# The bias of a spectral mixing, put into the PSUM bank by ScalarE instead of by a matmul

## The chip, the cores and the metric

The kernel runs on one core of a Trainium2 chip. The metric is the device time of one execution in microseconds (us). The kernel before took 1985.57 us, the median of three runs (1985.16 to 1986.27).

## What is computed

Three layers follow one another on a tensor of 4 batches, 3072 positions and 256 channels. The first takes a Fourier transform along the positions, mixes the channels of every frequency with a complex matrix and a bias, shrinks the result softly, and transforms back. The change lies in this layer alone. The reference, cut to it and to the order of the three:

```python
X = np.fft.rfft(x, axis=1)
Xr, Xi = X.real, X.imag
Yr = Xr @ w_r - Xi @ w_i + b_r
Yi = Xr @ w_i + Xi @ w_r + b_i
Yr = np.sign(Yr) * np.maximum(np.abs(Yr) - 0.01, 0.0)
Yi = np.sign(Yi) * np.maximum(np.abs(Yi) - 0.01, 0.0)
y = np.fft.irfft(Yr + 1j * Yi, n=3072, axis=1)
# y goes through moe (w_in, mish, w_out), then moe2 (w_k, relu squared, w_v, gate w_g)
```

## The kernel before

The program has two parts. `part1` is the Fourier layer, `part2` the other two layers. In both, every matrix product is made of products of high and low halves of its operands (names ending in h and l).

`part1` works on 48 blocks, 12 for each batch; a block is 128 frequencies of one batch. For block u TensorE does three groups of matmuls. `emit_F(u)` (F below) is the forward transform of 8 matmuls into the bank `xps`. `emit_M(u)` (M) is the mixing into the bank `yps`: 12 products and, last, one matmul of the constants `pick` and `bias` that adds the bias (L650). In every twelfth block (u = 0, 12, 24, 36, where `t` is 0) the mixing is split in two halves of 256 columns with a bias matmul each. `emit_I(u)` (I) is the inverse transform of 8 matmuls into `bps`. The order on TensorE in step u of the main loop (L736 to L800) is F(u+1), M(u), I(u-1).

ScalarE evacuates the banks. In step u it does, in this order: `post_M(u-1)` (reads `yps`, writes `yb`), `post_F(u+1)` (reads `xps`, writes `xh`), its share of decoding a weight, `post_I(u-2)` (reads `bps`, writes `bs`, which a DMA takes to `b_dr`), and in the last batch the share of a second weight. VectorE writes `xl` in `post_F` (called X below) and finishes `yb` in `post_M2` (called Y).

The weights of the later layers arrive as 64-bit floats and are decoded (`decode`, L446) in steps over both engines: VectorE `v0` (integer parts into `q`), ScalarE `sg` twice and `q`, VectorE `v1` (`q` times sign), ScalarE the high half, VectorE the low half. One piece is worked on per step for u from 6 to 14 (parked to DRAM through `wp` and `w_dr`) and two per step in the last batch (u from 36 on). Steps of different pieces overlap, so each `v1` waits for the `q` that ScalarE made just before.

VectorE also has work in the background, in a queue with a planner (`Background`, L353 to L410). It holds the butterflies before the transform of the next batch (tile `a`, due before that batch) and the butterflies after the inverse transform, called F3 here (tile `g`, two jobs of 48 entries for batch 0 in `part1`, one for each half of the channels, added at u = 16 and u = 20). The planner keeps a clock of its own in nanoseconds: TensorE's time `pe`, and VectorE's `bg.clock`. Ahead of each Y and X it emits background operations as long as their costs fit by its clock (`until`). A step of `pe` is 1710 for F, 2770 for M and 1710 for I (L767, L792, L796). Operations for `a` always go before those of F3 (`one`, `until`: `self.q or self.f3`). A new F3 job is loaded only when the job before it is empty, and may begin three steps after that (`step`, L368 to L374). What is left in the last batch is emitted at u = 46 (`drain`, L799), and then `load_y(0)` reads what F3 stored, for `part2`; `split_y` on VectorE comes after it and ahead of the last Y.

The order of each engine's instructions is the order in which this Python code emits them. SP issues all DMAs in one queue.

Of the kernel before, what the change touches and what calls it, by code (L numbers as in the profile page):

```python
# [10 lines left out]
F32 = mybir.dt.float32  # L11
F32R = mybir.dt.float32r
I32 = mybir.dt.int32
ACTF = mybir.ActivationFunctionType
# [15 lines left out]
NT = 12  # L30
# [83 lines left out]
def tile_fft_mix_moe_channel_mix(  # L114
# [23 lines left out]
    def pool(stack, name, bufs, **kw):  # L138
        return stack.enter_context(tc.tile_pool(name=name, bufs=bufs, reuse_waits="tile", **kw))
# [5 lines left out]
    def tt(o, a, b, op):  # L145
        V.tensor_tensor(out=o, in0=a, in1=b, op=op)  # L146
# [4 lines left out]
    def act(o, i, f, **kw):  # L151
        S.activation(out=o, in_=i, func=f, **kw)  # L152

    def mm(o, l, r, start, stop, **kw):
        T.matmul(out=o, lhsT=l, rhs=r, start=start, stop=stop, **kw)  # L155
# [97 lines left out]
    def both(a, z):  # L253

        return [e for pair in zip(a, z) for e in pair]
# [315 lines left out]
    def part1():  # L571
        with ExitStack() as es:
            c1 = pool(es, "c1", 1)
# [7 lines left out]
            psy = pool(es, "psy", 3, space=PSUM)  # L581
            psb = pool(es, "psb", 3, space=PSUM)

            fm, im = {}, {}
            bias = c1.tile([128, 512], F32R, name="bias")
            pick = c1.tile([128, 2, 128], F32R, name="pick")
            zero = c1.tile([128, 64], F32, name="zero")
            As = {}

            def new_a(b):  # L590
                As[b] = big.tile([128, 2, 32, 128], F32, tag="big", name="a")
                for h in range(2):
                    load_x(As[b], b, h)

            xt, ybt, xps, yps, bps = {}, {}, {}, {}, {}

            def emit_F(u):
                b, t = u // NT, ORD[u % NT]
                A = As[b]
                ps = psx.tile([128, 2, 256], F32, tag="x", name="xps")  # L600
                lr, li = LINES_F[t]
                line = lambda h, l: A[:, h, l, :]
                if b == 0 and t < 4:
                    line = lambda h, l: G0[:, 16 * h + LINES_G[l - 16], :]
                half = lambda z, i: z.rearrange("p (r i f) -> p r i f", r=2, i=2)[:, :, i, :]
                for h in range(2):
                    if t:
                        mm(ps[:, h, :], line(h, lr), fm[t][:, 0, :], True, False)
                        mm(ps[:, h, :], line(h, li), fm[t][:, 1, :], False, True)
                    else:  # L610
                        for i, l in enumerate((lr, li)):
                            mm(half(ps[:, h, :], i), line(h, l), half(fm[0][:, i, :], i), True, True)
                xps[u] = ps

            def post_F(u):
                t = u % NT
                ps = xps.pop(u)
                xh = xs_p.tile([128, 2, 256], F32R, tag="xh", name="xh")
                xl = xs_p.tile([128, 2, 256], F32R, tag="xl", name="xl")
                act(xh, ps, ACTF.Copy)  # L620
                tt(xl, ps, xh.bitcast(F32), SUB)
                xt[u] = (xh, xl)
                if t == 0:
                    zh = z_p.tile([128, 2, 256], F32R, tag="zh", name="zh")
                    zl = z_p.tile([128, 2, 256], F32R, tag="zl", name="zl")
                    for zz, xx in ((zh, xh), (zl, xl)):
                        S.activation(out=zz, in_=xx.bitcast(F32), func=ACTF.Copy)
                        S.activation(out=zz.rearrange("p h (r f) -> p (h r) f", r=2)[:, :, 0:1],
                                     in_=zero[:, 0:4].rearrange("p (a o) -> p a o", o=1), func=ACTF.Copy)
                    xt[u] += (zh, zl)  # L630

            def emit_M(u):
                t = u % NT
                ps = psy.tile([128, 512], F32, tag="y", name="yps")
                xs = xt.pop(u)
                if t:
                    groups = [(slice(0, 512), ((0, 256, 0), (1, 0, 0)))]
                else:

                    groups = [(slice(0, 256), ((0, 256, 0), (1, 0, 2))),  # L640
                              (slice(256, 512), ((0, 512, 2), (1, 256, 0)))]
                for gs, parts in groups:
                    n = gs.stop - gs.start
                    todo = []
                    for zl, lo in ((0, 0), (0, 1), (1, 0)):
                        for h in range(2):
                            w = wt["mix", h][lo]
                            for r, c0, z in parts:
                                todo.append((xs[z + zl][:, h, 128 * r:128 * r + 128], w[:, c0:c0 + n]))
                    todo.append((pick[:, 0 if t else 1, :], bias[:, gs]))  # L650
                    for i, (l, r) in enumerate(todo):
                        mm(ps[:, gs], l, r, i == 0, i == len(todo) - 1)
                yps[u] = ps


            def post_M(u):
# [69 lines left out]
            bg.add(both(z[8:], m[:4]) + m[4:])  # L726
            bg.flush()
            emit_F(0)
            post_F(0)
            bg.add(both(t0[0][1], t0[1][1]) + both(t0[0][2][:10], t0[1][2][:10]), 4)  # L730
            bg.add(both(t0[0][2][10:], t0[1][2][10:]), 8)
            NU = NB * NT

            pe, bg.clock = START
            x_at, y_at = bg.clock, 0.0
            for u in range(NU):  # L736
                b, t = divmod(u, NT)
                if t == NT - 1 and b + 2 < NB:
                    new_a(b + 2)
                if t == F1_AT[b] and b + 1 < NB:  # L740
                    hs = [f1_ops(As[b + 1], h) for h in range(2)]
                    for i, due in ((slice(14), 0), (slice(14, 24), 4), (slice(24, None), 8)):
                        bg.add(both(*[(h[0] + h[1])[i] for h in hs]), NT * (b + 1) + due)
                bg.jobs += F3_PART1.get((b, t), [])
                bg.step()
                if u == NU - NT - 1:
                    wt["in"] = big.tile([128, 2, 2, 2048], F32R, tag="big", name="win")
                    todo = [lambda: win_piece(0)]
                    for i in range(8):
                        if i < 7:  # L750
                            todo.append(lambda i=i: win_piece(i + 1))
                        todo.append(lambda i=i: wout_piece(i))
                    late = [lambda i=i: park_piece(i) for i in range(NPARK, 9)]
                    wq = Weights(todo[:6] + late + todo[6:])
                    wq.load(3)
                dec = 0
                if b == NB - 1:
                    dec = 2
                elif PARK_AT[0] <= u < PARK_AT[1]:
                    dec = 1  # L760
                    if u == PARK_AT[0]:
                        wq = Weights([lambda i=i: park_piece(i) for i in range(NPARK)])
                        wq.load(2)
                bg.flush(u + 1)
                if u == 6:
                    S.activation(out=mu1, in_=mu, func=ACTF.Copy, scale=-1.0, bias=1.0)
                pe += 1710 * (u + 1 < NU)  # L767
                if u + 1 < NU:
                    emit_F(u + 1)
                if u:  # L770
                    post_M(u - 1)
                if dec:
                    emit(wq.vec())
                    bg.clock += 2100
                if u:
                    bg.until(y_at + SLACK[0])
                    post_M2(u - 1)
                    y_at = bg.spend(y_at, 602)
                if u + 1 < NU:
                    bg.until(pe + 700 + SLACK[1])  # L780
                    post_F(u + 1)
                    x_next = bg.spend(pe + 700, 602)
                if dec:
                    emit(wq.sca(2))
                if u > 1:
                    post_I(u - 2)
                if dec == 2:
                    emit(wq.vec())
                    emit(wq.sca(2))
                    bg.clock += 2100  # L790
                emit_M(u)
                pe = max(pe, x_at + 300) + 2770  # L792
                y_new = pe + 700
                if u:
                    emit_I(u - 1)
                    pe = max(pe, y_at + 300) + 1710  # L796
                x_at, y_at = x_next, y_new
                if b == NB - 1 and t == 10:
                    bg.drain()  # L799
                    load_y(0)  # L800
# [267 lines left out]
```

## Time and profile before

| | us |
|---|---|
| median of three runs | 1985.57 |
| lowest, highest | 1985.16, 1986.27 |
| the profiled execution, its own time | 1985.22 |
| its span, first to last instruction | 1983.2 |
| TensorE busy in it | 1960.9 |
| VectorE busy | 1143.1 |
| ScalarE busy | 925.1 |

`part1` fills the first 327 us of the span, `part2` the rest. A busy share is a mean over stages with different limits; the ends of matmuls are modelled, so it is the distance from start to start that gives a matmul's price.

### The profile page before, as it was taken

How to read it: one execution, taken by the hardware profiler on the slowest of the kernel's cores; microseconds unless marked ns; L12 is line 12 of the kernel's file. 1: busy time of each engine (PE TensorE's matmuls, PEld its weight loads, DVE VectorE, ACT ScalarE, POOL GpSimd, SP SyncE). 2: the span in 40 equal slices, each digit the busy share in tenths (PEclk: the TensorE clock that was granted, in tenths of full speed). 3: DMA queues.
4: the chain of work that ended last, by engine and by line, in shares of the span. 5: the costliest groups of instructions: out<-in, count | busy, mean ns of one | idle time of the engine just before them, and what ended most of it. 6: DMA issues, size and time to landing. Idle time of an engine off the chain costs nothing.

```text
span 1983.2 us, 25749 instructions
## 1 busy us (share of the span) xinstructions
PE 1960.9 (99%) x10084; PEld 1687.4 (85%) x10084; DVE 1143.1 (58%) x2183; ACT 925.1 (47%) x1525; POOL 13.5 (1%) x28
## 2 busy tenths in 40 slices
PE   6999999999999999999999999999999999999999
PEld 5888888888888888888888888888888888888888
DVE  8999986655654764465375445555444543444444
ACT  2423286344444544444444445444443544444455
POOL 0000000000000000000000000000000000000000
PEclk9999999999999999999999999999999999999999
DMA  9445276011011010101101001011000000000000
GB/s 278 151 136 170 71 246 202 34 33 64 22 33 54 22 46 9 54 22 33 54 22 54 1 22 54 8 31 38 22 1 22 22 11 11 22 22 1 22 11 22
DMA packets 104553, 106.66 MB, mean 54 GB/s; under 512 B 7016, under 2 KB 85488, under 8 KB 103408
## 3 DMA queue, kind: packets, MB, share of 16 engines
q1 hardware_dynamic: 104432, 105.02, 16.7%
q8 instruction: 79, 1.29, 0.3%
q14 instruction: 42, 0.34, 0.1%
HBM read 62.53 MB, written 42.47 MB: 53 GB/s over the span
## 4 chain that ended last, share of the span: by engine, by line
PE 97%; DMA 1%; DVE 1%; ACT 1%; issue 0%; SPq 0%; DVEq 0%; ACTq 0%
PE a L155 26%; PE hps L155 26%; PE v L155 14%; PE kps L155 13%; PE yps L155 7%; PE bps L155 4%; PE xps L155 4%; PE zps L155 3%; DMA a<-in_x_dram 0%; DMA w_dr<-wp 0%; DMA wraw<-in_w_r_dram 0%; DMA im<-in_inv_dram 0%; ACT sg L152 0%; SPq L266 0%; DVE q L149 0%
## 5 line engine op out<-in xcount | busy, mean ns | idle before, releaser
L864 DVE CAST gh<-u 128x512 fp32r<-128x512 f32 x384 | 163.4, 425 | 685.1 <-PE a L155 594.3
L155 PE MATMUL a<-gh,wo 128*128 128x512 f32 x1536 | 536.7, 390 | 0.0
L155 PE MATMUL hps<-yh,win 128*128 128x512 f32 x1536 | 534.7, 389 | 0.0
L152 ACT ACTIVATE u<-hps 128x512 f32<-128x512 f32 x384 | 229.7, 598 | 483.1 <-PE hps L155 428.5
L155 PEld LDWEIGHTS hps<-yh,win 128*128 128x128 f32 x1536 | 288.4, 188 | 60.4
L155 PEld LDWEIGHTS a<-gh,wo 128*128 128x128 f32 x1536 | 288.6, 188 | 57.8
L155 PE MATMUL a<-gl,wo 128*128 128x512 f32 x768 | 300.1, 391 | 0.0
L155 PE MATMUL hps<-yl,win 128*128 128x512 f32 x768 | 298.8, 389 | 0.0
L155 PE MATMUL v<-b,kh 128*128 128x256 f32 x1536 | 279.8, 281 | 0.0
L146 DVE TENSOR_TENSOR gl<-u,gh 128x512 fp32r<-128x512 f32 x384 | 263.9, 687 | 3.6
L155 PEld LDWEIGHTS v<-b,kh 128*128 128x128 f32 x1536 | 249.6, 189 | 14.3
L155 PE MATMUL v<-b,kl 128*128 128x256 f32 x768 | 215.8, 281 | 0.0
L152 ACT ACTIVATE ka<-kps 128x512 f32<-128x512 f32 x192 | 114.8, 598 | 211.0 <-PE kps L155 210.9
L155 PEld LDWEIGHTS hps<-yl,win 128*128 128x128 f32 x768 | 144.2, 188 | 29.8
L155 PEld LDWEIGHTS a<-gl,wo 128*128 128x128 f32 x768 | 144.7, 188 | 25.7
L146 DVE TENSOR_TENSOR kl<-ka,kh 128x512 fp32r<-128x512 f32 x192 | 132.9, 692 | 44.0 <-ACT ka L152 29.4
L155 PE MATMUL kps<-xkl,wkt 128*128 128x512 f32 x384 | 150.7, 392 | 0.0
L155 PEld LDWEIGHTS v<-b,kl 128*128 128x128 f32 x768 | 144.2, 188 | 0.0
L155 PE MATMUL kps<-b,wkt 128*128 128x512 f32 x384 | 134.5, 391 | 0.0
L155 PE MATMUL kps<-xkh,wkt 128*128 128x512 f32 x384 | 134.0, 391 | 0.0
L152 ACT ACTIVATE ka<-ka 128x512 f32<-128x512 f32 x192 | 121.8, 634 | 6.1
L152 ACT ACTIVATE kh<-ka 128x512 fp32r<-128x512 f32 x192 | 121.6, 633 | 6.1
(80 smaller groups left out, 2069.8 us busy)
## 6 DMA issues: line engine op xcount, KB each, us to landing
b_dr<-bs SPq DMA_DIRECT2D x48, 256.0 KB, 2.2
g<-b_dr SPq DMA_DIRECT2D x8, 1536.0 KB, 6.7
y<-y_dr SPq DMA_DIRECT2D x48, 256.0 KB, 3.1
out_dram<-r SPq DMA_DIRECT2D x48, 256.0 KB, 2.2
y_dr<-g SPq DMA_DIRECT2D x80, 64.0 KB, 1.7
w_dr<-wp SPq DMA_DIRECT2D x9, 512.0 KB, 5.8
a<-in_x_dram SPq DMA_DIRECT2D x8, 512.0 KB, 6.2
y_dr<-g SPq DMA_DIRECT2D x32, 128.0 KB, 1.9
```

Source lines behind the costliest of these rows:

```text
L146: V.tensor_tensor(out=o, in0=a, in1=b, op=op)
L152: S.activation(out=o, in_=i, func=f, **kw)
L155: T.matmul(out=o, lhsT=l, rhs=r, start=start, stop=stop, **kw)
L864: return [lambda: V.tensor_copy(hi, u), lambda: tt(lo, u, hi.bitcast(F32), SUB)]
```

## The change

The matmul of `pick` and `bias` goes out of `emit_M`. In its place `pre_M(u)` fills the bank before M(u) begins: for the first three blocks with the same matmul, for the others with a ScalarE copy of a constant tile `full[0]` or `full[1]` (128 x 512, in SBUF). All products of M then add to what stands in the bank. The two constant tiles are made once, by two matmuls and two ScalarE copies between F(0) and `post_F(0)`. `pre_M(u+1)` stands at the end of step u's work on the bank of M, behind M(u) in the code; on ScalarE it is therefore the last instruction of step u. The planner's price of M goes from 2770 to 2550.

```diff
+            full = [c1.tile([128, 512], F32, name=f"full{i}") for i in range(2)]
...
+            def pre_M(u):
+                ps = yps[u] = psy.tile([128, 512], F32, tag="y", name="yps")
+                i = 0 if u % NT else 1
+                if u < 3:
+                    mm(ps, pick[:, i, :], bias, True, False, skip_group_check=True)
+                else:
+                    act(ps, full[i], ACTF.Copy)
+
             def emit_M(u):
                 t = u % NT
-                ps = psy.tile([128, 512], F32, tag="y", name="yps")
+                ps = yps[u]
...
-                    todo.append((pick[:, 0 if t else 1, :], bias[:, gs]))
                     for i, (l, r) in enumerate(todo):
-                        mm(ps[:, gs], l, r, i == 0, i == len(todo) - 1)
-                yps[u] = ps
+                        mm(ps[:, gs], l, r, False, i == len(todo) - 1, skip_group_check=True)
...
             emit_F(0)
+
+            for i in range(2):
+                ps = psb.tile([128, 512], F32, tag="b", name="cps")
+                mm(ps, pick[:, i, :], bias, True, True)
+                act(full[i], ps, ACTF.Copy)
             post_F(0)
...
+                if u == 0:
+                    pre_M(0)
                 emit_M(u)
-                pe = max(pe, x_at + 300) + 2770
+                if u + 1 < NU:
+                    pre_M(u + 1)
+                pe = max(pe, x_at + 300) + 2550
```

## Rows read from the trace of the kernel before

**Rows 1.** The page's part 4: the chain that ended last, by engine.
```profile
PE 97%; DMA 1%; DVE 1%; ACT 1%; issue 0%; SPq 0%; DVEq 0%; ACTq 0%
```

**Rows 2.** Windows: start:end, sum, busy us of each engine (instructions), granted clock, DMA.
```profile
0.00:16.00 16.00, 0.00 (x0) 0.00 (x0) 7.70 (x11) 2.44 (x3) 0.20 (x4) 1.00 0.90 257
...
220.00:240.00 20.00, 20.00 (x92) 17.08 (x91) 19.69 (x46) 5.43 (x10) 0.00 (x0) 1.00 0.20 64
...
300.00:320.00 20.00, 20.00 (x92) 17.11 (x91) 18.08 (x36) 18.72 (x38) 0.00 (x0) 1.00 0.44 143
```

**Rows 3.** Timeline of TensorE, block 3: start, us, line, operation [idle before].
```profile
44.59 0.39 PE L155 MATMUL yps<-bias,pick 128*128 128x512 f32 x1
44.82 1.89 PE L155 MATMUL bps<-im,yb 128*128 128x256 f32 x8
```

**Rows 4.** Timeline around the start of M(13): SP, TensorE, ScalarE.
```profile
90.78 8.43 SPq L266 DMA_DIRECT2D a<-in_x_dram  x10
...
105.12 1.28 PE L155 MATMUL yps<-wmh,xh 128*128 128x512 f32 x4
105.83 0.63 ACT L152 ACTIVATE wp<-q 128x512 fp32r<-128x512 f32 x1 [6.29 <-DMA w_dr<-wp]
...
106.85 0.59 ACT L152 ACTIVATE yb<-yps 128x512 f32<-128x512 f32 x1
```

**Rows 5.** Timeline of ScalarE, one step of the last batch (u = 44).
```profile
303.58 0.60 ACT L152 ACTIVATE xh<-xps 128x512 fp32r<-128x512 f32 x1
...
308.69 0.62 ACT L152 ACTIVATE q<-q 128x512 f32<-128x512 f32 x1
309.22 0.58 ACT L152 ACTIVATE yb<-yps 128x512 f32<-128x512 f32 x1
310.00 0.60 ACT L152 ACTIVATE xh<-xps 128x512 fp32r<-128x512 f32 x1 [0.20 <-PE xps L155]
```

**Rows 6.** Timeline of VectorE, the same step.
```profile
303.18 0.69 DVE L149 SCALAR_TENSOR_TENSOR q<-q,sg 128x512 f32<-128x512 f32 x1 [0.21 <-ACT q L152]
...
307.77 0.69 DVE L149 SCALAR_TENSOR_TENSOR q<-raw,q 128x512 int32<-128x512 int32 x1
...
309.34 0.69 DVE L149 SCALAR_TENSOR_TENSOR q<-q,sg 128x512 f32<-128x512 f32 x1 [0.28 <-ACT q L152]
```

**Rows 7.** Timeline of VectorE: first and last operations of the second F3 job, and after.
```profile
220.34 3.23 DVE L146 TENSOR_TENSOR g<-g 128x1024 f32<-128x1024 f32 x3
...
238.81 3.09 DVE L149 SCALAR_TENSOR_TENSOR g<-g 128x512 f32<-128x512 f32 x5
...
250.62 0.43 DVE L458 TENSOR_SCALAR q<-raw 128x512 int32<-128x512 int32 x1 [4.10 <-DMA raw<-in_moe_w_in_dram]
```

**Rows 8.** Timeline of the last batch: VectorE and ScalarE on parked weights.
```profile
282.02 0.68 DVE L146 TENSOR_TENSOR wp<-q,wp 128x512 fp32r<-128x512 f32 x1
...
288.55 0.63 ACT L152 ACTIVATE wp<-q 128x512 fp32r<-128x512 f32 x1 [1.11 <-DMA w_dr<-wp]
```

**Rows 9.** Timeline of TensorE: starts of M(37), M(46), I(46) with I(47).
```profile
257.80 1.28 PE L155 MATMUL yps<-wmh,xh 128*128 128x512 f32 x4
...
316.02 1.27 PE L155 MATMUL yps<-wmh,xh 128*128 128x512 f32 x4
...
323.86 3.61 PE L155 MATMUL bps<-im,yb 128*128 128x256 f32 x16
```

**Rows 10.** Timeline of VectorE at the end of `part1`: first split, last split, last Y.
```profile
321.63 0.43 DVE L568 CAST yh<-y 128x512 fp32r<-128x512 f32 x1 [0.94 <-DMA y<-y_dr]
...
323.15 0.69 DVE L146 TENSOR_TENSOR yl<-y,yh 128x512 fp32r<-128x512 f32 x1
...
324.69 0.69 DVE L149 SCALAR_TENSOR_TENSOR yb<-yps,yb 128x512 f32<-128x512 f32 x1 [0.84 <-ACT yb L152]
```

**Rows 11.** The page's part 6: DMAs, KB each, median us from issue to landing.
```profile
y<-y_dr SPq DMA_DIRECT2D x48, 256.0 KB, 3.1
...
y_dr<-g SPq DMA_DIRECT2D x80, 64.0 KB, 1.7
```

## The prediction, made before the changed kernel was run

> **What bounds the kernel now.** I read first the chain that ended last [rows 1]: TensorE is 97% of it, so time is what TensorE issues plus what it waits for. Then the windows of `part1` [rows 2]: TensorE is full in each of them, but it does not stand alone. VectorE is at 19.7 of 20 us before the last batch, and in the last batch ScalarE is at 18.7 and VectorE at 18.1 of 20. The change takes work from the engine that bounds and gives it to one that is nearly as full for a quarter of `part1`. So I then read the three engines' timelines in the places where one of them has no room.
>
> **What is taken away.** From the start of the bias matmul to the next matmul is 0.23 us [rows 3]. The three first blocks keep it, 45 lose it (the two halves of u = 12, 24, 36 counted as one): 45 x 0.23 = 10.4 us, if nothing else becomes late. By place: blocks 3 to 12 2.3 us, 13 to 36 5.5 us, 37 to 47 2.5 us.
>
> **What is added, and its price.** The trace of before has no ScalarE write to PSUM. The nearest rows are a copy-like step in SBUF, 0.62, and PSUM to SBUF, 0.58 to 0.60 [rows 5]; I take 0.60 until TensorE may start and 0.52 until ScalarE's next start (`q` to `yb`, 308.69 to 309.22 [rows 5]). The Trainium skill (ScalarE: Activation LUTs, "Step-by-step: what each stage is for") says that ScalarE writes faster to PSUM than to SBUF; no row here shows such a write. By it the copy would be at or below the lower end, and with 0.05 us less in each of twelve late steps the total falls by 0.6 us. The two matmuls and two copies that make `full` lie before M(0), which waits for other work of VectorE; I cost them at nothing, up to 0.5 us if that cover is gone.
>
> The copy for M(u+1) is ScalarE's last instruction in step u, and TensorE must have it to start M(u+1). So whatever ScalarE waits for in step u, TensorE now waits for too. That bites in four places.
>
> **Place 1, M(13).** In step 12 ScalarE waits 6.29 us for the landing of an earlier parked weight, until 105.83, and TensorE does not care: M(13) started at 105.12 [rows 4]. With the change bs(10) and the copy for M(13) queue behind that wait. From the landing to the end of the copy is 106.85 - 105.83 + 0.60 = 1.6 us. The landing is behind the loads of `a` at 90.78 on SP [rows 4], which follow the store of block 8, which follows F(11): M(3) to M(9) are ahead of that, so it comes 7 x 0.23 = 1.6 us earlier, at 104.2. M(13) starts at 105.9, where 102.8 (105.12 - 2.3) was due: 3.1 us are lost. Against before, M(13) is 0.8 us late. Bounds: the landing not moved at all, 2.4 late; moved by the whole 2.3, 0.1 late.
>
> **Blocks 13 to 36** then run at TensorE's pace: 0.8 - 5.5 = -4.7 us at M(37).
>
> **Place 2, the planner.** Each block's budget for background work shrinks by 220 ns, so I went through the planner's arithmetic with both constants, on paper as the code has it; I take from it only which operation stands in which step, no time. With 2770 it puts the second F3 job into steps 28 to 34, as the trace has it (220.34 to 241.9 [rows 7]). With 2550 the first job has 14 entries left at step 24; at step 25 the butterflies of batch 3 go ahead of them; the first job ends in step 32, the second is loaded in step 33 and may begin in step 36. There the last batch's decoding begins, and VectorE's spare time from 242 to 250 [rows 7] is unused. In the trace the second job takes 21.5 us, of which three X and three Y are 3.6 to 4.1 (0.60 to 0.69 each [rows 6, 7]): some 17.5 of its own. Shared out by the columns that the planner puts into each step, they fall as 6.0 into step 36, 0.4, 1.7, 0.3, 1.75, 0.8, 1.4, 0.6, 1.3, 0.6 into steps 37 to 45, and 2.5 into step 46 with the drain.
>
> Step 36 has room: the raw weights, whose landing VectorE awaited until 250.62 [rows 7], are no longer queued on SP behind that job's stores. There I add 0.2 us.
>
> **Place 3, steps 37 to 45.** ScalarE first: from xh at 303.58 to the start of yb at 309.22 it is never idle, 5.64; with the copy 0.52 and yb some 0.5 (0.78 to the next xh less 0.20 of waiting, less what two steps overlap) the step is 6.65, against TensorE's 6.19 (6.42 from xh to xh [rows 5] less 0.23). Even without F3 ScalarE becomes the bound. VectorE: its `v1` waits for ScalarE's `q` (309.34 [rows 6]) and the next `q` for the `v0` behind it, so the steps form a ring with Y and X in it. It took 6.16 (303.18 to 309.34), with 0.2 of slack, since the second `v0` ended at 308.46 and ScalarE took up `q` at 308.69 [rows 5, 6]: 6.0 us and what F3 adds, which stands between Y and X. A step takes the longer of 6.6 and 6.0 plus F3's share: 6.6, 7.7, 6.6, 7.7, 6.8, 7.4, 6.6, 7.2, 6.6 = 63.2. In step 41 the fourth parked weight waited 1.11 us for the second one's store [rows 8]; the second's low half (282.02) now comes after the delayed ring, and I add 1.4 more. Together 64.6 against 316.02 - 257.80 = 58.2 [rows 9]: 6.4 us lost. Bounds: 2.0 (ScalarE alone) to 8.
>
> **Place 4, the end of part1.** The job's last two operations come in step 46, at about 5 us after M(46) starts: `v1`, Y, two, X, low half, two, at the rates above. Their last stores are six DMAs issued one after the other, which I put at 2 us (ten loads of `a` took SP 8.43 [rows 4], larger ones); 1.7 to land, then the load of y with 3.1 [rows 11]: about 11.5 us after M(46). The second half's split takes 1.1 (0.43 and 0.69 [rows 10]), and the last Y queues behind it on VectorE: I(47) can start at 12.6 to 13. In the trace it starts half-way through the sixteen matmuls, some 325.6, which is 9.6 after 316.02 [rows 9]. I take 3.0 us lost (1.4 to 4.5). `part2` follows I(47) and moves with it.
>
> **The sum**, against the profiled execution: -4.7 + 0.2 + 6.4 + 3.0 = +4.9 us, 1985.2 to 1990.1. The median of the runs lies 0.35 above that execution: 1990.5 us.
>
> **The rivals.**
> - *All is hidden.* ScalarE has idle time on average (925 us busy), and the whole 10.4 us arrive: 1975.2. Against it: the place of the copy behind the wait in [rows 4]. Chance 0.06.
> - *Only ScalarE's queue bites.* Places 1 and 3 without F3's share, the tail hidden: -4.7 + 2.0 - 0.5 = -3.2, 1982.4. It needs VectorE to take 17 us more in 60 without being late, with 18.1 of 20 taken [rows 2]. Chance 0.13.
> - *F3 delays the steps, but its last store is in time*, or the reverse: -4.7 + 0.2 + 6.4 - 0.5 = +1.4, 1987.0. Chance 0.20.
> - *Forecast*: 1988 to 1993. It decides above 4.7 us lost in the last batch; from there the change is slower. Chance 0.52.
> - *TensorE slows after its waits.* It would wait some 4 us before I(47). The trace grants the full clock of 2.4 GHz also in the first 16 us, in which TensorE did nothing [rows 2], which speaks against a loss. If the clock fell to 1.2, I(47) and as much of `part2` would take twice their time: 1.7 to 3.4 us more, 1993.5. The Trainium skill (TensorE: Matmul & The Clock Gate, "Part 1: The HAM clock gate") has idle time lead to the lower level; row and skill differ here, and I go with the row. Chance 0.09.
> - *The copy is overwritten instead of added to.* The instructions and their waits would be the same, and so would the time; it has no chance of its own.
>
> **How the numbers follow.** 1982.5 to 1994.5 leaves out the first case and the outer edges of the second and the last. About 0.2%, 4 us, is what a measurement tells from no change: faster means below 1981.6, slower above 1989.5. Faster gets the first case and a part of the second, 0.09; same the rest of the second, the third, and the lower end of the forecast, 0.38; slower 0.53.
>
> **What would show it.** In the trace of after: an idle TensorE of some 3 us before M(13), released by ScalarE; the operations on `g` on VectorE between 245 and 325 and none from about 225 to 240; M starts 6.6 to 8 apart in the last batch, each released by the copy; the split of y late, and a gap before I(47). If M keeps 6.19 us through the last batch, or M(13) comes at 102.8, the argument on ScalarE's order is wrong; if F3 still ends before the last batch, that on the planner is.

## The result, and the profile after

The changed kernel took 1997.11 us, the median of six runs (1994.74 to 1999.45), against 1985.64 for the kernel before: a ratio of 1.0059 [1.0049, 1.0069] (in brackets, here and below, the 95% interval). It is slower, as forecast, but by 11.5 us where 4.9 were forecast, and 2.6 us above the range. The profiled execution took 1999.45 us (span 1997.4); it is the slowest of the six, so its trace holds some 2 us that the median does not.

The chain that ended last (the page's part 4), which answers [rows 1]: TensorE has 89% of it where it had 97%, and VectorE and DMAs came in.

```profile
PE 89%; DVE 5%; DMA 3%; ACT 1%; issue 1%; SPq 0%; DVEq 0%; ACTq 0%
```

The windows that answer [rows 2] (columns as there). VectorE's spare time is now between 220 and 240 us, 12.00 where it was full at 19.69. In the last batch TensorE is busy for 17.46 of 20. And in three windows the granted clock is below 1.00, which was nowhere so in `part1` before.

```profile
100.00:120.00 20.00, 16.31 (x67) 13.47 (x66) 11.63 (x38) 6.05 (x12) 0.00 (x0) 0.83 0.54 179
220.00:240.00 20.00, 20.00 (x92) 17.15 (x91) 12.00 (x22) 6.53 (x12) 0.00 (x0) 1.00 0.53 156
300.00:320.00 20.00, 17.46 (x76) 13.80 (x75) 17.98 (x34) 18.33 (x37) 0.00 (x0) 1.00 0.60 183
320.00:340.00 20.00, 14.13 (x58) 11.28 (x57) 11.70 (x22) 8.06 (x17) 0.10 (x1) 0.88 0.45 132
340.00:360.00 20.00, 20.00 (x85) 16.40 (x85) 8.32 (x16) 6.67 (x10) 0.00 (x0) 0.95 0.92 266
```

Where the 14.2 us between the two spans lie is read from the starts of M on TensorE's timeline in both traces; the forecast stands beside, cut at the same places:

| stretch | before | after | change | forecast |
|---|---|---|---|---|
| start to M(2) | 35.26 | 36.62 | +1.4 | +0.2 |
| M(2) to M(12) | 63.30 | 61.13 | -2.2 | -2.3 |
| M(12) to M(13) | 6.56 | 10.28 | +3.7 | +2.9 |
| M(13) to M(14) | 6.47 | 8.53 | +2.1 | -0.2 |
| M(14) to M(37) | 146.21 | 141.73 | -4.5 | -5.1 |
| M(37) to M(46) | 58.22 | 64.88 | +6.7 | +6.4 |
| M(46) to the first product of `part2` | 11.10 | 17.53 | +6.4 | +3.0 |
| from there to the end | 1656.1 | 1656.7 | +0.6 | 0 |

(The +0.2 at the start is no cost: M(2)'s own bias matmul stands ahead of its products now.) The first line is chance for the most part: the first matmul of the span came at 17.29 instead of 16.16, and over the thirteen profiles of this study it comes between 15.63 and 17.29, with 16.93 in a kernel that has nothing of the change (the last experiment).

**M(13)**, the timeline that answers [rows 4]: SP's loads, ScalarE's wait for the landing, `bs`, the copy, and M(13) and M(14). M(13) waits 3.69 us for the copy. Its first four products take 2.08 us, where M(14)'s take 1.28.

```profile
90.33 9.56 SPq L266 DMA_DIRECT2D a<-in_x_dram  x10
106.38 0.63 ACT L152 ACTIVATE wp<-q 128x512 fp32r<-128x512 f32 x1 [7.67 <-DMA w_dr<-wp]
106.91 0.58 ACT L152 ACTIVATE bs<-bps 128x512 f32<-128x512 f32 x1
107.39 0.59 ACT L152 ACTIVATE yps<-full 128x512 f32<-128x512 f32 x1
108.03 2.08 PE L155 MATMUL yps<-wmh,xh 128*128 128x512 f32 x4 [3.69 <-ACT yps L152]
...
116.56 1.28 PE L155 MATMUL yps<-wmh,xh 128*128 128x512 f32 x4
```

Short windows show the granted clock at its half level (1.2 GHz) behind this wait and behind the one before I(47), which comes below:

```profile
108.00:110.00 2.00, 1.97 (x5) 1.60 (x6) 1.47 (x6) 1.96 (x4) 0.00 (x0) 0.50 0.83 309
339.00:341.00 2.00, 2.00 (x7) 1.60 (x5) 0.00 (x0) 0.00 (x0) 0.00 (x0) 0.50 0.00 0
```

**The second F3 job**, SP's load of it and VectorE's operations, which answer [rows 7]: the first job ends at 229, the second is loaded at 235.94 and begins at 247.97, in the last batch. It began at 220.34 before.

```profile
226.24 3.09 DVE L149 SCALAR_TENSOR_TENSOR g<-g 128x512 f32<-128x512 f32 x5
...
235.94 0.32 SPq L277 DMA_DIRECT2D g<-b_dr  x1
...
247.97 1.22 DVE L146 TENSOR_TENSOR g<-g 128x1024 f32<-128x1024 f32 x1
249.80 5.02 DVE L146 TENSOR_TENSOR g<-g 128x1024 f32<-128x1024 f32 x12
```

**A step of the last batch** (ScalarE, with VectorE's `v1` and the M that the copy releases), which answers [rows 5, 6]. ScalarE's `q` waits 0.62 us for VectorE, the copy stands behind it, and M(43) behind the copy. From start to start the copy keeps ScalarE for 0.52 us (300.43 to 300.95) and releases TensorE 0.64 after its own start.

```profile
299.89 0.63 ACT L152 ACTIVATE q<-q 128x512 f32<-128x512 f32 x1 [0.62 <-DVE q L149]
300.43 0.58 ACT L152 ACTIVATE yps<-full 128x512 f32<-128x512 f32 x1
300.56 0.69 DVE L149 SCALAR_TENSOR_TENSOR q<-q,sg 128x512 f32<-128x512 f32 x1
300.95 0.58 ACT L152 ACTIVATE yb<-yps 128x512 f32<-128x512 f32 x1
301.07 1.20 PE L155 MATMUL yps<-wmh,xh 128*128 128x512 f32 x4 [0.85 <-ACT yps L152]
```

**The end of `part1`**, which answers [rows 9 to 11]: M(46), the last stores of F3, the load of y, the second split, the last Y, I(47) behind a wait of 5.09, and the first product of `part2`.

```profile
323.17 1.20 PE L155 MATMUL yps<-wmh,xh 128*128 128x512 f32 x4 [0.78 <-ACT yps L152]
...
327.98 2.92 SPq L291 DMA_DIRECT2D y_dr<-g  x6
...
330.95 1.49 SPq L554 DMA_DIRECT2D y<-y_dr  x2
...
335.67 0.43 DVE L568 CAST yh<-y 128x512 fp32r<-128x512 f32 x1 [0.69 <-DMA y<-y_dr]
...
336.74 0.68 DVE L149 SCALAR_TENSOR_TENSOR yb<-yps,yb 128x512 f32<-128x512 f32 x1
337.48 3.78 PE L155 MATMUL bps<-im,yb 128*128 128x256 f32 x8 [5.09 <-DVE yb L149]
340.70 0.99 PE L155 MATMUL hps<-yh,win 128*128 128x512 f32 x1
```

### The profile page after: what moved, and what is told of

Read it like the earlier page. It is cut to its first block, busy times and chain, and to the rows that moved or that the text cites. A ratio compares the mean times of both kernels' runs of the same rounds, so it can differ in the third digit from the quotient of the medians.

```text
span 1997.4 us, 25685 instructions
## 1 busy us (share of the span) xinstructions
PE 1959.2 (98%) x10037; PEld 1681.7 (84%) x10037; DVE 1142.4 (57%) x2183; ACT 946.5 (47%) x1572; POOL 13.0 (1%) x28
## 4 chain that ended last, share of the span: by engine, by line
PE 89%; DVE 5%; DMA 3%; ACT 1%; issue 1%; SPq 0%; DVEq 0%; ACTq 0%
PE a L155 26%; PE hps L155 26%; PE v L155 13%; PE kps L155 13%; PE zps L155 3%; PE yps L155 3%; PE bps L155 2%; PE xps L155 2%; DVE a L146 1%; DVE q L149 1%; DVE yb L149 1%; DVE a L149 1%; DVE g L146 1%; DVE xl L146 0%; DMA raw<-in_moe_w_out_dram 0%
## 5 line engine op out<-in xcount | busy, mean ns | idle before, releaser
L155 PEld LDWEIGHTS v<-b,kh 128*128 128x128 f32 x1536 | 249.6, 189 | 14.3
```

## The experiments

The runs come in three groups, each on one chip together with the kernel before, whose medians there were 1986.05, 1985.97 and 1985.8 us; ratios are to the one of the same group.

### The change's two halves, one at a time

First the copies with the planner's old constant:

```diff
-                pe = max(pe, x_at + 300) + 2550
+                pe = max(pe, x_at + 300) + 2770
```

> The change with the planner's price of M put back to 2770; the ScalarE copy stays last in its step. Theory (order of ScalarE, F3's slip, and TensorE's clock after long waits are separate costs): F3's second job is back in steps 28 to 34, so the spacing of M in the last batch falls from 6.5 to 8.2 us to 6.5 to 6.7 (ScalarE alone bounds it), no late last store, no 5 us wait before I(47) and no half clock there; the wait and the half clock at M(13) stay. 1985.5 to 1988.5 us. Rival (the copies themselves cost, the planner does not matter): it stays near 1997.

Measured: 1985.67 us (1984.56 to 1986.19), ratio 0.9997 [0.9988, 1.0006]. The copies alone, at the end of ScalarE's step, neither gain nor lose: of 10.4 us nothing arrives. M(13) still waits, and from M(37) to M(46) it takes 60.44 us, 2.2 more than before (forecast for ScalarE alone: 2.0). That the two sums agree is in part luck: eight of the nine steps take 6.5 to 6.6, 0.8 more than before in all, and the ninth takes 7.87, because M(42) waits 1.41 us for a copy that stands behind the landing of a parked weight (ScalarE waits 1.16), as M(13) does.

```profile
106.26 0.63 ACT L152 ACTIVATE wp<-q 128x512 fp32r<-128x512 f32 x1 [6.55 <-DMA w_dr<-wp]
...
107.92 1.20 PE L155 MATMUL yps<-wmh,xh 128*128 128x512 f32 x4 [2.57 <-ACT yps L152]
```

Then the constant alone, in the kernel before, bias matmul and all:

```diff
-                pe = max(pe, x_at + 300) + 2770
+                pe = max(pe, x_at + 300) + 2550
```

> The kernel before, bias matmul and all, with 2550 in place of 2770 and nothing else. Theory: F3's second job slips into the last batch here too; VectorE bounds its steps (6.4 to 7.7 us from M to M), the last store, the load of y and the last Y come late, and I(47) waits 3 to 5 us, with a half clock after it: 1991 to 1996 us. M(13) shows no wait. Rival: without the copies the last batch absorbs F3, within 2 us of 1985.6.

Measured: 2001.58 us (2000.17 to 2002.41), ratio 1.0076 [1.0061, 1.0091]. One number, and no instruction added or removed, costs 15.5 us, more than the whole change, and far above the 1991 to 1996 expected. From M(37) to M(46) it takes 66.2 us, 8.0 more than before; TensorE waits there for Y, not for a copy (the view of its waits: total, times, longest, in `part1`), and the clock falls at the end.

```profile
PE bps L155 <- DVE yb L149: 8.7, 5, 3.7
...
320.00:340.00 20.00, 16.28 (x62) 13.22 (x63) 12.95 (x25) 7.85 (x16) 0.10 (x1) 0.86 0.45 131
340.00:360.00 20.00, 20.00 (x80) 16.30 (x80) 7.84 (x14) 6.36 (x10) 0.00 (x0) 0.89 0.78 239
```

So the loss is the planner's, and the copies on top of it give some 4 us back (15.5 less 11.5). That the last batch loses more here than in the changed kernel (8.0 against 6.7) lies in its last step: from M(45) to M(46) it is 10.83 us, with a wait of 2.45 before I(45) and a granted clock of 0.84, against 7.27 in the changed kernel; the eight steps before take 55.4 against 57.6. What makes that one wait no run took apart.

### Is the clock a cause of its own? Spare matmuls in the two long waits

The changed kernel, with matmuls that nobody reads ahead of M(13) (15) and I(47) (20):

```diff
+            def filler(n):
+                ps = psb.tile([128, 512], F32, tag="b", name="fps")
+                for i in range(n):
+                    mm(ps, pick[:, 0, :], bias, True, True)
...
+                if u == 13:
+                    filler(15)
...
+            filler(20)
             emit_I(NU - 1)
```

> The changed kernel, with spare matmuls whose result nobody reads ahead of two blocks that wait: 15 ahead of M(13) and 20 ahead of I(47), each 128 x 128 by 128 x 512 into a PSUM tile of their own. What is computed for the output is unchanged. Theory 'TensorE slows after its waits': in the changed kernel M(13) to M(14) took 8.53 us where its neighbours take 6.19, and I(47)'s eight matmuls took 3.2, both after waits of 3.69 and 5.09 us. With the waits filled, both blocks still start when ScalarE's copy and VectorE's Y let them, but the granted clock stays at its full level: M(13) to M(14) 6.2 and I(47) to its end 1.6. That is 2.3 + 1.6 = 3.9 us less than the changed kernel's 1997.1, 1993.2 (1992 to 1994.5). Rival 'the slow stretch is not made by the wait' (the matmuls there are slow for another reason, as contention for PSUM with the copy): nothing changes, 1996.5 to 1998.

Measured: 1995.29 us (1995.03 to 1995.69), ratio 1.0046 [1.0031, 1.0061]: less is saved than expected (1992 to 1994.5). In the traces, though, the theory holds to two tenths: M(13) starts where it did (108.14 against 108.03), but M(14) comes 6.06 us later instead of 8.53, and I(47) takes 1.65 us to the first product of `part2` instead of 3.22: 4.0 us, and 4.0 is the difference of the spans (1993.4 against 1997.4).

```profile
104.50 3.79 PE L155 MATMUL fps<-bias,pick 128*128 128x512 f32 x15
...
108.14 1.14 PE L155 MATMUL yps<-wmh,xh 128*128 128x512 f32 x4
...
114.20 1.27 PE L155 MATMUL yps<-wmh,xh 128*128 128x512 f32 x4
...
335.61 1.99 PE L155 MATMUL bps<-im,yb 128*128 128x256 f32 x8 [0.55 <-DVE yb L149]
337.26 0.58 PE L155 MATMUL hps<-yh,win 128*128 128x512 f32 x1
```

The medians differ by 1.8 only. The executions of the changed kernel lie 4.7 us apart and those with the fillers 0.7, and the mean granted clock of each execution goes the same way: 0.999 in the fastest of the changed kernel (1994.74), 0.998 in the next two, 0.997 in the three slowest, and 1.000 in all four with the fillers. So the changed kernel loses more to the clock in some executions than in others, and its trace is of the one that took longest; at which wait the others lose less is not shown. The share of the clock in the median is thus 2 to 4 us.

### The end of `part1`: the split behind the last Y

The changed kernel with the split of y moved (on VectorE it stood ahead of the last Y):

```diff
-            for h in range(2):
-                emit(split_y(0, h)[1])
             post_M(NU - 1)
             post_M2(NU - 1)
+            for h in range(2):
+                emit(split_y(0, h)[1])
```

> The changed kernel, with the split of y into its high and low parts moved behind the last Y and X on ScalarE and VectorE (it stood ahead of them). Theory: I(47) started at 337.48 because VectorE's last Y queued behind the second half of the split, which waited 4.52 us for the load of y. With the order turned, I(47) follows M(47) at about 334 and what starts part2 waits for the split alone (335.67 + 0.69 + one product): the first product of part2 at about 337, 3.5 us earlier than the 340.70 of the changed kernel, 1993.6 (1992.5 to 1995). TensorE still waits for the split, so part of the half clock may stay: up to 1995.5. Rival: the load of y alone sets the start of part2, with I(47) hidden behind it in either order: 1996.5 to 1998.

Measured: 1993.22 us (1990.33 to 1994.78), ratio 1.0034 [1.0022, 1.0046], 3.9 us less than the changed kernel. I(47) follows M(47) at once, and what is late is the split alone.

```profile
326.53 3.61 PE L155 MATMUL bps<-im,yb 128*128 128x256 f32 x16
...
330.56 0.49 PE L155 MATMUL hps<-yh,win 128*128 128x512 f32 x1 [0.42 <-DVE yh L568]
```

From M(46) at 319.20 to there it is 11.4 us, 6.2 less than in the changed kernel's trace and 0.3 more than in the kernel before; `part2` then loses about 1.0 to its first waits for the split. (In this one execution M(13) also waited less, 2.14 us, and did not slow down; that is why its span is shorter than the medians say.)

### M(13): the landing, and the place in ScalarE's queue

The changed kernel with the parking of weights one step earlier, and nothing else:

```diff
-PARK_AT = (6, 15)
+PARK_AT = (5, 14)
```

> The changed kernel with only one thing moved: the first parking of weights begins one step earlier (PARK_AT 5 and 14 for 6 and 15). Copies stay the last instruction of ScalarE's step, the planner stays at 2550. Theory 'place 1': M(13) waits only because the copy queues behind the landing of the last parked weight. With the landing earlier, M(13) starts 6.2 us after M(12) instead of 10.3, no half clock follows, M(14) comes 6.2 later instead of 8.5, and all of it reaches the end: 6.4 us less than in the changed kernel's trace, 1991.0 to 1993.5. Rival 'the copy at the end of the step is late anyway': M(13) still waits more than 2 us for the copy, 1995.5 to 1998.

Measured: 1992.4 us (1991.59 to 1993.66), ratio 1.0033 [1.002, 1.0045], 4.7 us less than the changed kernel. ScalarE meets no wait for a landing there any more, and M(13) starts 6.33 us after M(12), M(14) 6.22 after that (103.66, 109.88).

Next the copy itself earlier in ScalarE's step, right behind `post_M(u-1)`, with the planner's constant at 2770:

```diff
                 if u:
                     post_M(u - 1)
+                else:
+                    pre_M(0)
+                if u + 1 < NU:
+                    pre_M(u + 1)
...
-                if u == 0:
-                    pre_M(0)
                 emit_M(u)
-                if u + 1 < NU:
-                    pre_M(u + 1)
-                pe = max(pe, x_at + 300) + 2550
+                pe = max(pe, x_at + 300) + 2770
```

> As e1 (2770), and the copy for M(u+1) moved ahead on ScalarE: behind the evacuation of M(u-1), before that of F(u+1) and before the decoding. Theory: M(13) no longer waits for the landing of a parked weight and the clock does not fall there, so blocks 3 to 36 give their 7.8 us; the last batch loses up to 3 us because ScalarE has more work than a step is long, though a lag is now absorbed in part. 1978 to 1982 us. Rival (what delays M(13) is not the place in ScalarE's queue but the wait for an engine as such): as e1.

Measured: 1982.65 us (1981.62 to 1986.25), ratio 0.9983 [0.9974, 0.9992]: 3.4 us faster than before, less than expected. M(13) no longer waits. But the same landing holds Y on both engines, I(12) waits for Y, and M(14) is late instead, 8.05 us behind M(13):

```profile
104.22 1.28 PE L155 MATMUL yps<-wmh,xh 128*128 128x512 f32 x4
106.51 0.63 ACT L152 ACTIVATE wp<-q 128x512 fp32r<-128x512 f32 x1 [5.95 <-DMA w_dr<-wp]
...
108.15 0.69 DVE L149 SCALAR_TENSOR_TENSOR yb<-yps,yb 128x512 f32<-128x512 f32 x1 [0.28 <-ACT yb L152]
108.90 1.99 PE L155 MATMUL bps<-im,yb 128*128 128x256 f32 x8 [1.56 <-DVE yb L149]
```

The same with the bias matmul kept for blocks 36 to 45, where ScalarE is full:

```diff
-                if u < 3:
+                if u < 3 or 36 <= u < 46:
```

> As e3, and blocks 36 to 45, where ScalarE decodes two weights per step, keep their matmul in place of the copy (blocks 46 and 47 have the copy). Theory: the last batch runs at 6.41 us per step as in the kernel before, and 35 blocks give 0.23 us each: 8.0 us, 1977.5 to 1979.5. Rival (ScalarE's load in the last batch costs nothing): as e3 or slower than it by 2.3 us.

Measured: 1982.55 us (1981.04 to 1985.1), ratio 0.9983 [0.9974, 0.9993]: a miss. It is no better than the run before it, with the same stalls at the same landings: M(13) to M(14) 8.4, M(36) to M(37) 7.6, M(42) to M(43) 8.17. What ScalarE waits for was still in the way. Its load counts too, but comes out even here: with the copies in the last batch (the run before) the first three steps from M(37) take 6.2 us each and the last three 6.6, with the matmuls the first five take 6.4 each, and from M(37) to M(46) it is 59.1 against 58.9. The early copy and the earlier parking together:

> The run e3 (the changed kernel with the copies one place earlier on ScalarE and the planner's budget back at 2770), with the first parking of weights one step earlier (PARK_AT 5 and 14 for 6 and 15), so that the last parked weight's buffer is stored ahead of the loads of batch 2 on SP instead of behind them. Theory: in e3 M(13) to M(14) took 8.05 us because I(12) waited for Y, which queued on VectorE and ScalarE behind the landing of that weight's buffer (106.51). With the landing out of the way it takes 6.2: 1.8 us less than e3's 1982.65, 1980.8 (1980 to 1981.5). Rival: the landing isn't what holds M(14), or the earlier parking makes another step late by the same: 1982 to 1984.

Measured: 1980.97 us (1979.7 to 1982.3), ratio 0.9973 [0.9964, 0.9983], as expected: M(13) at 102.78, M(14) at 108.99.

### All landings out of the way

The run with the kept matmuls, the parking earlier, the raw weights of the last batch loaded from step 33 instead of 35, the four late parks laid between other pieces, and the bias tiles loaded by DMAs (of its edits, only those to the last batch's weights are shown):

```diff
...
+                if u == NU - NT - 3:
                     todo = [lambda: win_piece(0)]
...
-                    wq = Weights(todo[:6] + late + todo[6:])
+                    t, k = todo, late
+                    wq = Weights(t[:5] + [k[0], t[5], k[1], t[7], k[2], t[9], k[3], t[6], t[8]]
+                                 + [t[11], t[10], t[12], t[13]] + t[14:])
...
```

> The run e4 (copies one place earlier on ScalarE, planner's budget 2770, the bias matmul kept for blocks 36 to 45) with four stalls for DMA landings taken away: the parking of weights one step earlier, the two tiles of the bias loaded by DMAs in place of two matmuls and two copies at the start, the raw weights of the last batch loaded two steps earlier, and the four late parks laid between other pieces of work. Theory 'the gain is there, and landings take it': 35 blocks give 35 x 0.23 = 8.0 us; e4 kept 3.5 of it, and lost 0.8 at the start, 2.2 after M(13), 1.4 at M(36) to M(37) and 1.6 to 2 at M(42) to M(43). With these gone: 1977.5 to 1979.5. Rival 'the gain is capped by VectorE or ScalarE': what one stall gives back is taken by the next wait, 1981.5 to 1983.

Measured: 1982.39 us (1980.39 to 1983.82), ratio 0.998 [0.9971, 0.999]. The rival's number, but not its reason. The stalls at M(13), M(36) and M(42) are gone; the six new DMAs for the bias tiles (the expectation says eight) made one of their own. They hold SP from 30.34 to 39.76 us, and batch 1's loads of `a` start behind them at 39.81 (28.82 in the run before it). The first weight landed late, and TensorE waited behind block 5, with half clock after it:

```profile
59.83 0.67 ACT L152 ACTIVATE sg<-raw 128x512 int32<-128x512 f32 x1 [4.61 <-DMA raw<-in_moe_w_k_dram]
...
61.64 3.49 PE L155 MATMUL bps<-im,yb 128*128 128x256 f32 x8 [4.11 <-DVE yb L149]
```

So the tiles went back to two matmuls and two copies, now behind M(1):

> The run e8 with its one new stall undone. In e8 the two bias tiles came by eight DMAs on SP ahead of batch 1's loads and the first weights to be parked, and TensorE waited 4.11 us behind block 5 for Y (which queued behind the weight's landing), with 2.2 us of half clock after it: M(5) to M(6) 12.53 instead of 6.19. Here the tiles are made by two matmuls and two copies again, but behind M(1), where TensorE is at its full clock (0.46 us on TensorE). Theory 'the gain is there, and landings take it': no wait of more than 0.5 us is left in part1, 35 blocks give 8.0 us less 0.5: the first product of part2 at 319 us, and 1978.3 (1977.3 to 1979.3). Rival 'each stall that is taken away comes back elsewhere': 1981 to 1983, as e3, e4 and e8.

Measured: 1977.23 us (1976.98 to 1978.12), ratio 0.9956 [0.9942, 0.9971]: 8.6 us faster than the kernel before, with 35 copies that are worth 35 x 0.23 = 8.0, and just below the 1977.3 to 1979.3 expected. After the start no wait of TensorE is left in `part1`; the window of the last batch, where the bias matmul stays, is full, and the first product of `part2` comes at 319.25, where it came at 327.12.

```profile
300.00:320.00 20.00, 20.00 (x91) 16.86 (x91) 14.26 (x28) 14.21 (x30) 0.24 (x1) 1.00 0.38 118
...
319.25 0.58 PE L155 MATMUL hps<-yh,win 128*128 128x512 f32 x1
```

Its control is the kernel before with the same three moves of landings and no copy:

> The kernel before, bias matmul and all, with the three moves of landings that e8 and e9 have: first parking one step earlier, raw weights of the last batch loaded two steps earlier, late parks laid between other pieces. The control for e9. Theory: in the kernel before TensorE hides these landings, so the moves alone give nothing: 1985.0 to 1986.6. Rival: the moves by themselves make up part of what e9 gains: 1982 to 1984.5.

Measured: 1984.94 us (1984.33 to 1985.87), ratio 0.9996 [0.9986, 1.0005]. The moves alone give nothing that can be told from zero: where the bias stays on TensorE, TensorE hides those landings. Against this control the copies gain 7.7 us. Two kernels were not run: this one with the copies in blocks 36 to 45 too, and one with all landings moved and the copy still last in ScalarE's step. So how much of the gain needs the early place, once the landings are gone, is not shown.

## Why the prediction missed, step by step

**Right: ScalarE's order.** M(13) waits, released by the copy, for the reason given; removing the landing and nothing else gave 4.7 us back.

**Right: the planner.** The second F3 job left the stretch from 220 to 240, was loaded in step 33 and began in step 36; its last operations came in step 46. The nine steps from M(37) took 6.5, 7.7, 6.6, 7.9, 6.8, 7.3, 6.6, 8.2 and 7.3 us against 6.6, 7.7, 6.6, 7.7, 8.2, 7.4, 6.6, 7.2 and 6.6. The rule "the longer of 6.6 and 6.0 plus F3's share" held for the first four to a tenth or two. The sum, 64.9 against 64.6, is better than its parts: the 1.4 put into step 41 for the parked weight did not appear, and steps 44 and 45 took 1.7 more. In these two VectorE's ring waited for the landing of raw weights, 0.94 and 0.59 us, which it did in no step there before and which the rule has no term for:

```profile
308.81 0.43 DVE L458 TENSOR_SCALAR q<-raw 128x512 int32<-128x512 int32 x1 [0.94 <-DMA raw<-in_moe_w_out_dram]
...
316.67 0.43 DVE L458 TENSOR_SCALAR q<-raw 128x512 int32<-128x512 int32 x1 [0.59 <-DMA raw<-in_moe_w_out_dram]
```

That two errors cancel is luck. The 1.4 for the parked weight came in step 41 of the copies alone, where no F3 stands in the way (above). That VectorE's share decides and not the copies is shown by the constant alone (8.0 us) and the copies alone (2.2).

**Wrong: the clock, as a rival at 0.09 and in I(47) only.** The step that failed is "The trace grants the full clock of 2.4 GHz also in the first 16 us, in which TensorE did nothing [rows 2], which speaks against a loss." There is no matmul in that row, so its 1.00 is evidence of nothing. The trace of the changed kernel has the same column at 1.00 while F(1) runs slowly: eight matmuls of one shape take 2.81 us in F(1), after an idle start, and 1.89 in F(2).

```profile
22.64 2.81 PE L155 MATMUL xps<-fm,g 128*128 128x256 f32 x8
...
28.63 1.89 PE L155 MATMUL xps<-fm,g 128*128 128x256 f32 x8
...
16.00:24.00 8.00, 5.28 (x14) 3.92 (x15) 7.94 (x23) 3.80 (x10) 0.00 (x0) 1.00 0.98 326
```

After its waits of 3.69 and 5.09 us TensorE ran at a granted clock of 0.50 (the short windows above). The Trainium skill (TensorE: Matmul & The Clock Gate, "Part 1: The HAM clock gate") has an idle TensorE fall to the lower level, and these rows agree with it where the prediction set it aside. The rival also looked at one wait. The forecast had TensorE wait 3.1 us at M(13), and that wait costs most: 2.3 us there and 1.6 at I(47), in the trace 3.9 of the 8.7 us between forecast and measured up to `part2`. The spare matmuls gave 4.0 back. But the clock does not carry the miss alone: with them the kernel still took 1995.29 us, above the forecast's range. Of the other 4.8 us, 1.8 lie in the end of `part1` and 0.9 in the landing (both below), 1.2 in the start, which is chance for the most part, and 0.9 in the stretches from M(14) to M(46).

**Mis-sized: the end of `part1`.** I(47) was put at 12.6 to 13 us after M(46) and came at 14.3: the six last stores took SP 2.92, not 2, and the last Y's own 0.7 us, from its start to I(47)'s, was not in the sum. With the clock, 6.4 us were lost where 3.0 were forecast. The mechanism was right: with the split behind the last Y, 3.9 us came back.

**Mis-sized: the landing at M(13).** It was forecast to come 1.6 us earlier than before, and came 0.55 later (106.38 against 105.83): the loads on SP began 0.45 earlier, in an execution that started 1.1 late, and took 9.56 instead of 8.43. That is 0.9 us of M(12) to M(13).

**Right: the copy's price and the start.** The 45 copies take 0.61 us in the median (the view of one tile, `yps`: min/median/max), against 0.60 taken.

```profile
L152 ACT ACTIVATE yps<-full x45: 580/607/625, 38.0 to 325.7; 128x512 f32<-128x512 f32 x45
```

Against 0.62 from SBUF to SBUF [rows 5] they are 0.01 faster. The Trainium skill (ScalarE: Activation LUTs, "Step-by-step: what each stage is for"), which the prediction weighed, has ScalarE write faster to PSUM than to SBUF; the rows show this 0.01 of it, which the total does not feel. The tiles of the bias cost nothing in the changed kernel: from the first matmul to M(2) it is 19.33 us, and 19.10 before, of which 0.23 is M(2)'s bias. In the other runs with that start it is 19.1 to 20.4, without it 19.1 to 19.5, so up to 1 us can hang on it.

**The range.** It was to hold the outer edges of its cases, but the clock's case was reckoned as an addition of 3.4 at most to I(47), and the terms at M(13) and I(47) had no common bad end: 1994.5 plus 2.3 at M(13) would have held 1996.8, just short of the median. The sign was right for the reason given, the planner's slip: the copies alone changed nothing (1985.67).

## What to carry to other kernels

Work that leaves the engine that bounds must also leave the queues that engine depends on: a copy put last in ScalarE's step made TensorE wait for everything ScalarE waits for, and the same copy, in 35 of the 45 blocks, gave 8.6 us once it stood behind the read of the bank before it and DMA landings were moved out of its way. A constant in a planner is a change of its own and is timed alone: here it cost 15.5 us by pushing one job into the stretch where its engine was full. And a column that reads full speed where the engine did nothing is no evidence; the price of a wait is the wait and the slow matmuls after it.

## What the runs showed of the hardware

- The lower clock after a wait was not expected. After waits of 3.69 and 5.09 us TensorE's matmuls took nearly twice their time (I(47)'s eight 3.78 instead of 1.99), and the granted clock there is 0.50, the half level (1.2 GHz of 2.4). After 2.57 us (copies alone) and 2.14 (split moved) they did not slow down; after 2.45 us in the run with the constant alone eight matmuls took 3.08. The length of one wait alone does not say whether the clock falls.
- Six DMAs of 0.5 MB in all held SP's queue for 9.4 us at the start, and what was queued behind them stalled TensorE for 4.11 us twenty microseconds later, at a block where it had no wait in the other profiles.
